# Feature tiles of the bias stage: 54 of 144 on GpSimd, 66 on VectorE, 24 on ScalarE

## The chip, the cores and the metric

The kernel runs on one core of a Trainium2 chip. A core has engines that run side by side, each with its own queue of instructions in a fixed order: TensorE (PE; its weight loads are listed apart as PEld), VectorE (DVE), ScalarE (ACT), GpSimd (POOL) and SyncE (SP), which here only issues DMA transfers. They wait for one another by semaphores. Matrix products go to PSUM, everything else lies in SBUF (both 128 partitions wide); DMA engines move data between SBUF and DRAM. The metric is device time in microseconds, taken as a median of runs; a profile of one further execution shows when each instruction ran.

## What is computed

An attention layer with a learned position bias, followed by a soft mixture of experts, all in float32. The shapes are 8 batches, 8 heads, 576 positions and 64 numbers a head. What the change touches is the bias:

```python
rel = pos[:, None] - pos[None, :]
psi_rel = log1p(abs(rel))
psi_i = log1p(maximum(pos[:, None], 1.0))
x = (psi_rel / psi_i)[..., None]          # 576 x 576 x 1
h = maximum(x @ w1 + b1, 0.0)             # 32 hidden numbers for each pair
bias = h @ w2                             # one number a head for each pair
scores = scores + bias.transpose(2, 0, 1)[None]
```

The scores then go through a softmax over the last axis and are multiplied by v; the result, 4608 rows of 512, is dispatched to 32 slots of 8 experts (two matrix products with a ReLU between), and combined again. The bias is the same for all batches, so it is computed once.

## The kernel before

**Bias stage.** The first 54 us make the bias for all heads. For a position i the hidden vector depends on the distance alone: `relu(log1p(distance) * (w1 / psi_i) + b1)`. One *feature tile* holds this for four positions (32 partitions each) and for as many distances as are needed, n of them:

- `tabs` is a table of log1p of the distances 0 to 575, the same on all partitions, loaded once; `scl` holds w1 / psi_i as a column for each tile; `cols[:, 1]` is b1, and `nb1` is -b1.
- `bias_feats(i)` (L226) makes the four tiles t = 0 to 3 of group i, that is of 16 positions. Two forms are in use: ScalarE computes `relu(scl * tabs + b1)` (L236), VectorE computes `max(scl * tabs, -b1)` (L239). The second is the first less b1; the constant that this leaves out is added later, by `bcon`, of which `bias_group` picks the column that suits the group.
- There are 36 groups: 8 in each of four blocks of 128 positions, whose biases go to `bias_m`, and 4 for the last 64 positions, which go to `bias_r`. The length n = max(base + 16, 576 - base) falls from 576 to 304 and rises again, in steps of 16 from group to group.
- `bias_group` (L245) first makes the features up to three groups ahead (`AHEAD = 3`), then multiplies the four tiles of its own group by `wbd`, which holds w2 (L260; each tile fills its own 32 columns of TensorE, in two or three pieces), lets ScalarE move the 128 x 591 result from PSUM to a tile `e` with the constant added (L264), and issues the write of `e` to DRAM on SyncE's queue (L265).
- Features and results share one pool, `wp`, of 24 buffers. A feature's buffer is free when its products are done, a result's when its write has landed. PSUM is used in four pairs of banks in turn.

Before the change ScalarE makes tile t = 0 of five groups in six (30 tiles) and VectorE everything else (114). GpSimd has nothing to do until the attention stage.

**Reading the bias back.** `load_bias(hp, c)` (L298, its DMAs at L296) reads block c of a pair of heads, shifted row by row, into SBUF: three transfers each for blocks 0 to 3 (`bm`), two for the last (`br`). They are issued on the same SyncE queue as the writes. For the first pair of heads they are in this stage, and each has to wait until the writes of its block have landed. In this stage the order of instructions on each queue, and the choice of buffers, is made by the framework's scheduler from the program's order and its own estimates; it puts the reads of a block between later writes.

**Attention and the rest.** Thirty-two units (4 pairs of heads, 8 batches) follow in an order written out by hand (`PLAIN` and `END`), under which no instruction changes place. A unit takes five rows of 128 queries; the names of its steps are S (scores, L370 and L366), t (bias added and minimum taken, L383, on VectorE), e (exponential, L390), m (sums, L398 and L399), n (normalisation by GpSimd, L312, a `tensor_scalar` of 128 x 576), T and R (transposes, L348), M (product with v, L473). Row 4 holds the last 64 queries of both heads and reads `br`; in the first unit its step t comes before that of row 3. The mixture of experts runs within the last units and after them. L655 and L653 belong to it, and are VectorE's work on 128 x 160 and 128 x 5 numbers.

Of the kernel before, what the change touches and what calls it, by code (L numbers as in the profile page):

```python
# [13 lines left out]
ALU = mybir.AluOpType  # L14
# [111 lines left out]
def body(ctx, tc, qk, v, wcol, phi, mw1, mw2, tabh, consth, out, outr):  # L126
    nc = tc.nc
# [56 lines left out]
    tabs = xp.tile([P, tabh.shape[1]], F32, name="tabs", tag="xo")  # L184
# [6 lines left out]
    scl = xp.tile([P, NJ], F32, name="scl", tag="xk")  # L191
# [15 lines left out]
    nb1 = const.tile([P, 1], F32, name="nb1")  # L207
# [3 lines left out]
    for g in range(4):  # L211
        rs = slice(32 * g, 32 * g + 32)
        nc.vector.tensor_scalar(out=wbd[rs, H * g:H * g + H], in0=cols[rs, 2:2 + H], scalar1=1.0 / QS, scalar2=None,
                                op0=ALU.mult)
# [11 lines left out]
    def bias_feats(i):  # L226
        bases, scales, _ = jobs[i]
        fb = [None] * 4
        relu = [False] * 4
        for t in range(4):  # L230
            sc = scales[t]
            n = max(bases[0] + 16, S - bases[0])
            f = fb[t] = wp.tile([P, S], F32, name="f", tag="w")[:, 0:n]
            relu[t] = t == 0 and i % 6 != 5
            if relu[t]:
                nc.scalar.activation(out=f, in_=tabs[:, 0:n], func=AF.Relu, bias=cols[:, 1:2],  # L236
                                     scale=scl[:, sc:sc + 1])
            else:
                nc.vector.tensor_scalar(out=f, in0=tabs[:, 0:n], scalar1=scl[:, sc:sc + 1], scalar2=nb1[:, 0:1],  # L239
                                        op0=ALU.mult, op1=ALU.max)  # L240
        feats[i] = fb, relu

    nb = [0]
# [1 line left out]
    def bias_group():  # L245
        i = nb[0]
        nb[0] += 1
        for j in range(i if i else 0, i + AHEAD + 1):
            if j < len(jobs) and j not in feats:
                bias_feats(j)  # L250
        bases, scales, dst = jobs[i]
        fb, relu = feats[i]
        pb = ps(i % 4)

        i0 = bases[0] + 16
        cuts = sorted({0, i0, 512, S + 15})
        for c0, c1 in zip(cuts, cuts[1:]):
            for t in (1, 2, 3, 0):
                x = fb[t][:, i0 - c1:i0 - c0][:, ::-1] if c0 < i0 else fb[t][:, c0 - i0 + 1:c1 - i0 + 1]
                nc.tensor.matmul(pb[32 * t:32 * t + 32, c0 // 512, c0 % 512:(c1 - 1) % 512 + 1], wbd, x, start=True,  # L260
                                 stop=True, tile_position=(0, 32 * t))
        e = wp.tile([P, S + 15], F32, name="e", tag="w")
        bc = bcon[:, 1 * relu[0] + 2 * relu[3]:1 * relu[0] + 2 * relu[3] + 1]
        nc.scalar.activation(out=e, in_=pb.rearrange("a x n -> a (x n)")[:, 0:S + 15], func=AF.Identity, bias=bc)  # L264
        nc.sync.dma_start(out=dst, in_=e)  # L265
# [54 lines left out]
    for i, x in enumerate(END.split()):  # L320
        n, u = x.rstrip("+").split("/")
# [707 lines left out]
```

## Time and profile before

| | us |
|---|---|
| median of 3 runs (606.54 to 610.15) | 607.62 |
| the profiled execution | 607.81 |
| its span, first to last instruction | 605.4 |
| busy: TensorE / ScalarE / VectorE / GpSimd | 582.2 / 469.8 / 414.9 / 224.6 |
| feature tiles on VectorE (114), first start to last end | 47.9 |

In the rows of the profile a line stands as L and its number, `out<-in` names the tiles written and read, and `x` the number of instructions. A group's row gives busy time in us and the mean of one instruction in ns, then the idle time of the engine before these instructions and what ended it. A row of the timeline gives start and duration in us, with runs of like instructions merged (the duration is then that of the run); in brackets stand the idle time before and who ended it. SPq is SyncE's queue issuing a DMA; when the transfer lands is told elsewhere. An instruction's duration can reach into that of the next one on its engine. The rows that matter are shown in the prediction.

### The profile page before, as it was taken

What the parts mean: (1) busy time and instruction counts of PE and PEld (TensorE: products, weight loads), DVE (VectorE), ACT (ScalarE), POOL (GpSimd) and SP (SyncE); (2) the same over time, 40 slices, a digit from 0 to 9 for tenths busy, and PEclk for the clock granted to TensorE, in tenths of its full rate; (3) what the DMA queues carried; (4) which work ended last, traced back from release to release, by engine and by line L of the source; (5) the groups of instructions that cost most, each with busy time, mean ns of one, the idle gap of its engine ahead of it and who ended that gap; (6) DMA issues with size and microseconds to landing.
All of it is one profiled execution on the core that took longest, in us unless ns stands there. A gap on an engine that the chain in (4) does not pass through costs nothing.

```text
span 605.4 us, 18911 instructions
## 1 busy us (share of the span) xinstructions
PE 582.2 (96%) x7423; PEld 370.5 (61%) x7423; DVE 414.9 (69%) x1320; ACT 469.8 (78%) x974; POOL 224.6 (37%) x336
## 2 busy tenths in 40 slices
PE   6998899999999999999999999999999999999993
PEld 4874666666666666666666666665666666653551
DVE  7997767667676667667676667677679788852233
ACT  6996888888888888888888888887877887751233
POOL 0001644455555544455555544544233422400000
PEclk9999899999999999999999999999999999999998
DMA  6778222333855544675444356522332145689997
GB/s 223 272 243 298 66 84 84 109 101 123 242 183 190 174 156 154 216 251 175 138 156 138 120 203 222 164 75 73 123 123 71 55 129 210 207 331 324 410 381 316
DMA packets 41897, 110.73 MB, mean 183 GB/s; under 512 B 7120, under 2 KB 7248, under 8 KB 41808
## 3 DMA queue, kind: packets, MB, share of 16 engines
q1 hardware_dynamic: 41808, 109.52, 53.2%
q8 instruction: 58, 0.95, 0.7%
q14 instruction: 31, 0.25, 0.1%
HBM read 82.10 MB, written 27.41 MB: 181 GB/s over the span
## 4 chain that ended last, share of the span: by engine, by line
PE 83%; DMA 6%; DVE 4%; ACT 3%; issue 1%; POOL 0%; SPq 0%; DVEq 0%; ACTq 0%; POOLq 0%
PE ps L473 25%; PE ps L370 21%; PE ps L348 17%; PE ps L260 7%; PE ps L366 6%; DMA wt<-in_moe_w_dram 5%; ACT y L390 2%; PE ps L539 1%; DMA xo<-xs 1%; PE ps L669 1%; PE ps L888 1%; DVE ob L315 1%; PE ps L921 1%; DVE y L383 0%; POOL y L312 0%
## 5 line engine op out<-in xcount | busy, mean ns | idle before, releaser
L312 POOL TENSOR_SCALAR y<-y,sm 128x576 f32<-128x576 f32 (+1 forms) x320 | 221.9, 707 | 302.1 <-DVE sm L399 246.6
L383 DVE CUSTOM_DVE_ANT_0 y<-ps,bm 128x576 f32<-128x576 f32 x256 | 185.3, 754 | 95.5 <-PE ps L348 55.2
L390 ACT ACTIVATE y<-y,mn 128x576 f32<-128x576 f32 x288 | 222.1, 772 | 28.3 <-DVE sm L398 19.3
L315 ACT COPY at<-ps 128x1024 f32<-128x1024 f32 (+3 forms) x211 | 153.9, 732 | 37.0 <-PE ps L348 28.3
L473 PE MATMUL ps<-at,v 128*64 128x320 f32 (+1 forms) x1280 | 176.4, 415 | 0.0
L370 PE MATMUL ps<-qk 64*128 64x288 f32 x1024 | 155.6, 421 | 0.1
L348 PEld LDWEIGHTS ps<-ident,y 64*128 64x128 f32 x2624 | 103.1, 139 | 56.5 <-POOL y L312 16.0
L348 PE MATMUL ps<-ident,y 64*128 64x64 f32 x2624 | 118.0, 226 | 4.1 <-POOL y L312 3.6
L473 PEld LDWEIGHTS ps<-at,v 128*64 128x64 f32 x1280 | 84.0, 137 | 60.7 <-issue 10.8
L370 PEld LDWEIGHTS ps<-qk 64*128 64x128 f32 x1024 | 90.8, 188 | 26.7 <-DVE sm L398 9.8
L390 ACT ACTIVATION_READ_ACCUMULATOR y<-y,mn 128x1 f32 x288 | 53.9, 187 | 0.0
L260 PE MATMUL ps<-f,wbd 128*32 128x79 f32 (+32 forms) x856 | 48.4, 345 | 1.7 <-DVE f L239 1.6
L239 DVE TENSOR_SCALAR f<-tabs,scl,nb 128x576 f32<-128x576 f32 (+17 forms) x114 | 47.9, 496 | 0.5 <-DMA tabs<-in_tab_dram 0.5
L315 DVE COPY at<-ps 128x256 f32<-128x256 f32 (+3 forms) x77 | 33.8, 442 | 15.3 <-PE ps L348 13.8
L260 PEld LDWEIGHTS ps<-f,wbd 128*32 128x32 f32 x856 | 33.2, 112 | 16.9 <-issue 8.1
L366 PE MATMUL ps<-qk 64*64 64x288 f32 x256 | 38.0, 415 | 0.0
L315 DVE COPY xts<-ps 128x256 f32<-128x256 f32 (+1 forms) x57 | 25.9, 455 | 12.1 <-PE ps L473 12.1
L264 ACT ACTIVATE e<-ps,bcon 128x591 f32<-128x591 f32 x36 | 26.7, 754 | 4.7 <-DMA bias_m<-e 2.1
L399 DVE RECIPROCAL sm<-sm 128x2 f32<-128x2 f32 (+1 forms) x160 | 26.5, 165 | 5.5
L398 DVE TENSOR_SCALAR sm<-sm 128x2 f32<-128x2 f32 (+1 forms) x160 | 28.3, 177 | 2.9 <-ACT y L390 2.3
L383 DVE CUSTOM_DVE_ANT_0 y<-ps,br 128x576 f32<-128x576 f32 x32 | 24.0, 750 | 1.9 <-PE ps L348 1.1
L383 DVE DVE_READ_ACCUMULATOR2_ANT mn<- 128x1 f32 x288 | 24.1, 84 | 0.0
(144 smaller groups left out, 333.5 us busy)
## 6 DMA issues: line engine op xcount, KB each, us to landing
wt<-in_moe_w_dram SPq DMA_DIRECT2D x63, 512.0 KB, 6.1
qk<-in_qk_dram SPq DMA_DIRECT2D x32, 608.0 KB, 3.8
v<-in_v_dram SPq DMA_DIRECT2D x32, 320.0 KB, 3.2
bias_m<-e SPq DMA_DIRECT2D x32, 295.5 KB, 4.2
out_dram<-ob SPq DMA_DIRECT2D x16, 512.0 KB, 5.9
xs<-xts SPq DMA_DIRECT2D x24, 288.0 KB, 4.9
xo<-xs SPq DMA_DIRECT2D x8, 864.0 KB, 5.4
bm<-bias_m SPq DMA_DIRECT2D x16, 288.0 KB, 4.4
```

The costliest lines, as they stand in the source:

```text
L239: nc.vector.tensor_scalar(out=f, in0=tabs[:, 0:n], scalar1=scl[:, sc:sc + 1], scalar2=nb1[:, 0:1], op0=ALU.mult, op1=ALU.max)
L260: nc.tensor.matmul(pb[32 * t:32 * t + 32, c0 // 512, c0 % 512:(c1 - 1) % 512 + 1], wbd, x, start=True, stop=True, tile_position=(0, 32 * t))
L264: nc.scalar.activation(out=e, in_=pb.rearrange("a x n -> a (x n)")[:, 0:S + 15], func=AF.Identity, bias=bc)
L312: nc.gpsimd.tensor_scalar(out=out, in0=y, scalar1=r, scalar2=1.0, op0=ALU.mult, op1=ALU.mult)
L315: (nc.vector.tensor_copy if eng else nc.scalar.copy)(out=out, in_=in_)
L348: nc.tensor.matmul(out, src[rs], ident[rs, rs], is_transpose=True, start=True, stop=True, tile_position=(64 * r, 0))
L366: nc.tensor.matmul(pss[0].t[rs, n, 0:HALF], x[rs, 1152:1216], x[rs, 64 + n * HALF:64 + (n + 1) * HALF], start=True, stop=True, tile_positi ...
L370: nc.tensor.matmul(pss[hh].t[:, n, 0:HALF], x[rs, 640 + p * P:640 + (p + 1) * P], x[rs, k0:k0 + HALF], start=True, stop=True, tile_positio ...
L383: nc.vector.tensor_tensor_reduce(out=d["y", p][:, hs].rearrange("a (x n) -> a x n", x=2), in0=t[:, :, 0:HALF], in1=biases[hp][p][:, hs].re ...
L390: nc.scalar.activation(out=y, in_=y, func=AF.Exp, bias=d["mn", p][:, hh:hh + 1], scale=-1.0, accum_out=d["sm", p][:, hh:hh + 1])
L398: nc.vector.tensor_scalar(out=r, in0=r, scalar1=1e-9, scalar2=None, op0=ALU.add)
L473: nc.tensor.matmul(po[64 * hh:64 * hh + 64], d["v"][:, v0:v0 + 64], main[:, :, 4 * hh + i, :] if i < 4 else rest, start=i == 0, stop=i == ...
```

## The change

Three tile positions are handed out anew in `bias_feats`. Tile t = 3 of every group, and tile t = 2 of every even group, is made by GpSimd, with the same `tensor_scalar` as VectorE's. ScalarE makes t = 0 in two groups of three in place of five of six; in the third, VectorE makes it. So GpSimd has 36 + 18 = 54 tiles, ScalarE 24, and VectorE 36 + 18 + 12 = 66. Everything else is as it was: lengths, products, results, writes, the pool of buffers.

```diff
-            relu[t] = t == 0 and i % 6 != 5
+            relu[t] = t == 0 and i % 3 != 2
             if relu[t]:
                 nc.scalar.activation(out=f, in_=tabs[:, 0:n], func=AF.Relu, bias=cols[:, 1:2],
                                      scale=scl[:, sc:sc + 1])
             else:
-                nc.vector.tensor_scalar(out=f, in0=tabs[:, 0:n], scalar1=scl[:, sc:sc + 1], scalar2=nb1[:, 0:1],
-                                        op0=ALU.mult, op1=ALU.max)
+                eng = nc.gpsimd if t == 3 or t == 2 and i % 2 == 0 else nc.vector
+                eng.tensor_scalar(out=f, in0=tabs[:, 0:n], scalar1=scl[:, sc:sc + 1], scalar2=nb1[:, 0:1], op0=ALU.mult,
+                                  op1=ALU.max)
```

## The prediction

> **What bounds the kernel now.** I read the page first, for the instructions that the change touches.
>
> ```profile
> span 605.4 us, 18911 instructions
> ...
> L239 DVE TENSOR_SCALAR f<-tabs,scl,nb 128x576 f32<-128x576 f32 (+17 forms) x114 | 47.9, 496 | 0.5 <-DMA tabs<-in_tab_dram 0.5
> ```
>
> VectorE's 114 feature tiles fill 47.9 us with no gap after the first: 47.9 / 114 = 0.42 us from one to the next (the mean of 496 ns is longer, since each instruction begins some 76 ns before the last one is recorded as ended). Next come the busy times of the stage by stretches; behind the length stand PE, PEld, DVE, ACT and POOL, then clock, DMA share and GB/s.
>
> ```profile
> 10.00:20.00 10.00, 10.00 (x209) 7.75 (x201) 10.00 (x24) 9.63 (x15) 0.00 (x0) 1.00 0.58 221
> 20.00:30.00 10.00, 10.00 (x203) 8.16 (x203) 10.00 (x28) 9.50 (x17) 0.00 (x0) 1.00 0.82 290
> 30.00:40.00 10.00, 10.00 (x202) 7.77 (x196) 10.00 (x26) 9.72 (x17) 0.00 (x0) 1.00 0.79 273
> 40.00:50.00 10.00, 10.00 (x163) 5.18 (x160) 10.00 (x24) 8.28 (x12) 0.00 (x0) 1.00 0.71 221
> ```
>
> VectorE never rests, GpSimd never works, ScalarE is nearly full. TensorE shows full too, but its records overlap and it consumes what VectorE hands over. So VectorE sets the pace of the features. A second chain runs beside it: SyncE's queue, which writes each group's result to DRAM and reads the biases of the first head pair back.
>
> ```profile
> 22.27 0.32 SPq L296 DMA_DIRECT2D bm<-bias_m  x1
> ...
> 33.17 0.32 SPq L296 DMA_DIRECT2D bm<-bias_m  x1
> ...
> 44.29 0.32 SPq L296 DMA_DIRECT2D bm<-bias_m  x1
> ...
> 55.47 1.31 SPq L296 DMA_DIRECT2D bm<-bias_m  x3
> 59.31 1.15 SPq L296 DMA_DIRECT2D br<-bias_r  x2
> ```
>
> Each of the first four is the first read of a block of eight groups (`bm`), and the last row reads the rest (`br`). A read waits at the head of the queue until the last write of its block has landed, and later writes wait behind it:
>
> ```profile
> SPq L296 <- DMA bias_m<-e: 9.8, 6, 4.2
> ```
>
> The blocks follow one another at 10.9, 11.1 and 11.2 us. In between the DMA engines are full (share 1.01 to 1.04; columns as above):
>
> ```profile
> 24.00:31.00 7.00, 7.00 (x150) 5.86 (x152) 7.00 (x21) 6.70 (x12) 0.00 (x0) 1.00 1.01 380
> 35.00:42.00 7.00, 7.00 (x134) 4.85 (x132) 7.00 (x18) 6.76 (x12) 0.00 (x0) 1.00 1.03 391
> ...
> 50.00:54.00 4.00, 4.00 (x60) 2.14 (x58) 2.50 (x6) 2.32 (x4) 0.00 (x0) 1.00 1.04 403
> ```
>
> So this chain runs at the pace of the transfers and of the queue's waits, and it is slower than the features: eight groups cost VectorE 8 x 114 / 36 x 0.42 = 10.6 us. Where the two meet is seen on VectorE in the first attention unit:
>
> ```profile
> 55.09 0.76 DVE L383 CUSTOM_DVE_ANT_0 y<-ps,bm 128x576 f32<-128x576 f32 x1 [2.59 <-PE ps L370]
> ...
> 62.70 0.76 DVE L383 CUSTOM_DVE_ANT_0 y<-ps,br 128x576 f32<-128x576 f32 x1 [0.30 <-DMA br<-bias_r]
> ```
>
> The unit starts when the features are done (55.09), yet its row at 62.70 waits 0.30 us for the last bias read. **The end of the stage is set twice**, by the features and, 0.30 us later, by the DMA chain. What follows is one fixed order of work on a full TensorE, so I carry a shift of that row to the end one for one.
>
> **The change, part by part.** VectorE loses 48 tiles, ScalarE loses 6, GpSimd gets 54. A tile's length is max(base + 16, 576 - base), 304 to 576, on average 440 over any of the three engines' shares. Their prices by length:
>
> ```profile
> L239 DVE TENSOR_SCALAR f<-tabs,scl,nb 128x576 f32<-128x576 f32 x7 | 3.6, 571 | 0.5 <-DMA tabs<-in_tab_dram 0.5
> ...
> L239 DVE TENSOR_SCALAR f<-tabs,scl,nb 128x304 f32<-128x304 f32 x7 | 2.5, 426 | 0.0
> ```
> ```profile
> L312 POOL TENSOR_SCALAR y<-y,sm 128x576 f32<-128x576 f32 x288 | 212.3, 750 | 256.0 <-DVE sm L399 227.0 <-PE ps L348 5.3 <-DVE sm L398 4.6
> L312 POOL TENSOR_SCALAR y<-y,sm 128x64 f32<-128x64 f32 x32 | 10.3, 322 | 46.1 <-DVE sm L399 19.6 <-ACT y L390 7.9 <-ACT at L315 6.3
> ```
>
> VectorE: 145 ns over 272 columns, 0.533 ns a column, so 0.23 us of streaming at 440 in its 0.42. GpSimd: 428 ns over 512 columns, 0.836 ns a column and 268 ns fixed, so 0.636 us at 440; back to back each begins 27 ns early (two in 1.47 below), so 0.61. L312 also has two scalar operations with a column operand, and I take its price for the new tiles.
>
> If the two engines did not disturb each other, GpSimd would need 54 x 0.61 = 32.9 us, VectorE 66 x 0.42 = 27.7, and ScalarE 60 instructions (24 tiles, 36 results) at 9.63 / 15 = 0.64, 38.5 us. ScalarE would bind: 9.4 us less than 47.9. That is the lower bound. But they do disturb each other. Small VectorE operations in the attention stage show it:
>
> ```profile
> L398 DVE TENSOR_SCALAR sm<-sm x160: 144/160/921, 57.6 to 525.4; 128x2 f32<-128x2 f32 x128, 128x1 f32<-128x1 f32 x32
> L655 DVE TENSOR_TENSOR ck<-ck,km x8: 325/326/614, 457.8 to 547.7; 128x160 f32<-128x160 f32 x8
> ```
> ```profile
> 406.88 0.54 DVE L398 TENSOR_SCALAR sm<-sm 128x2 f32<-128x2 f32 x1 [0.60 <-ACT y L390]
> ...
> 482.58 0.17 DVE L653 TENSOR_SCALAR km<-km 128x5 f32<-128x5 f32 x1
> ...
> 483.01 0.45 DVE L655 TENSOR_TENSOR ck<-ck,km 128x160 f32<-128x160 f32 x1
> ```
> ```profile
> 406.65 1.47 POOL L312 TENSOR_SCALAR y<-y,sm 128x576 f32<-128x576 f32 x2
> ...
> 482.52 1.55 POOL L312 TENSOR_SCALAR y<-y,sm 128x576 f32<-128x576 f32 x2 [0.82 <-DVE sm L399]
> ```
>
> At 406.88 an operation of 0.16 us lasts 0.54: it ends at 407.42, some 0.02 us after the first of the two GpSimd instructions (406.65 + 0.75). It got in between the two, and the pair took no longer for it. At 483.01 a longer one (160 columns) ends 0.17 us after the first GpSimd instruction, and the pair takes 1.55 in place of 1.47. So VectorE waits out a running GpSimd instruction, then streams, and about the first 0.1 us of the next GpSimd instruction is free of the conflict. A feature tile that has waited streams 0.23 + 0.02 = 0.25 us after GpSimd's end and delays the next GpSimd instruction by about 0.15. A pair, one tile on each, thus takes 0.61 + 0.15 = 0.76 us. With 54 pairs and 12 more VectorE tiles: 54 x 0.76 + 12 x 0.42 = **46.1 us, 1.8 less than 47.9**.
>
> The upper bound is no overlap at all: 54 x 0.636 + 66 x 0.42 = 62.1 us, 14.2 more. I choose the pair price, since it is read from the same GpSimd instruction; the bounds stay for the range. The Trainium skill, SBUF — State Buffer, "Who interferes with whom", has the harder rule: a float32 `tensor_scalar` between SBUF tiles can take both VectorE ports, one of them is GpSimd's, and whichever instruction comes first holds it whole while the other "fully blocks". The trace agrees that VectorE waits out GpSimd (921 against 160 ns), but not that the next GpSimd instruction gives up its whole length; by the rule the sum would be the upper bound.
>
> ScalarE's 6 tiles less save 6 x 0.64 = 3.8 us on an engine that is not the one that ends the stage: nothing by itself. TensorE and the writes keep their work; a group still needs four tiles.
>
> **Where the 1.8 us go.** The DMA chain starts with the eighth group's write (the read at 22.27 waits for it). Groups 0 to 7 are long (mean 520 columns): before, 25 VectorE tiles at 0.277 + 0.185 = 0.46, 11.5 us; after, 12 pairs at 0.68 + 0.20 = 0.88 and 2 tiles more, 11.4 us. The chain starts where it did, its blocks are paced by full DMA engines, and the `br` read lands where it did. The features' gain comes later, in the short middle groups, and turns into a longer wait at the 62.70 row: 0.30 becomes some 2 us. If features came later, only 0.30 us of cover exists; beyond it the cost is one for one.
>
> Sum: -0.1 (the chain's start) on a profiled execution of 607.81 us, which is 2.4 over its span; the median of the runs shown is 0.2 below it, so 607.81 - 0.1 - 0.2 = **607.5 us**. Its own range, with the chain's start moving by up to 2 us either way, is 605 to 610.
>
> **The rivals.** *Slower: the two engines exclude each other more than the small rows show.* Place: every pair of the stage. It decides from a pair price of (47.9 + 0.3 - 5.0) / 54 = 0.80 us on, only 0.04 above mine. If GpSimd's free 0.1 us is lost, a pair is 0.61 + 0.25 = 0.86, the features take 51.4 us, and the time is 607.6 + 3.2 = 610.8; at the upper bound it is 607.6 + 14.2 - 0.3 = 621.5. For it: the small operations hold VectorE for nanoseconds, a feature tile for a quarter of a microsecond, and two VectorE tiles in a row may keep GpSimd out. Against it: the 406.65 pair, which let VectorE in at no cost. 0.21, about half of it near each end. The rule of the Trainium skill's SBUF page is the case of the far end.
>
> *Faster: the DMA chain shortens too.* ScalarE, 9.63 of 10 us busy at 10 to 20, has one tile less before the eighth group, and the order of SyncE's queue in this stage is the framework's plan, not written by hand; if the plan lets one more write go ahead of each read, each of four blocks saves a write of 302 KB at 391 GB/s, 0.77 us. With that tile's 0.64 us: 3.7 less, 603.9 us, if the features keep up, which needs pairs of (47.9 - 3.7 - 5.0) / 54 = 0.73 us. For it: full DMA engines only between waits. Against: nothing in the change touches the queue's code. 0.16.
>
> *The new wait is for buffers.* Features and results share 24 buffers, and a result's is free only when its write has landed; ScalarE already waited for that:
>
> ```profile
> 50.32 1.40 ACT L264 ACTIVATE e<-ps,bcon 128x591 f32<-128x591 f32 x2 [1.86 <-DMA bias_m<-e]
> ```
>
> If a GpSimd tile gets such a buffer, GpSimd's later tiles queue behind it, TensorE waits for them, and ScalarE for TensorE: 1.9 us in each of three blocks, 607.6 + 5.6 - 0.3 = 613. Against: no feature tile waited so before. 0.06.
>
> **How the numbers follow.** Forecast 0.57, exclusion 0.21, shorter chain 0.16, buffers 0.06. About 0.5% (3 us) is what a measurement can tell from no change. The forecast lies within it; the shorter chain is beyond it; exclusion (from 610.8 on) and buffers are slower: faster 0.16, same 0.57, slower 0.27. The range, 603 to 617, leaves out the upper half of the exclusion (0.11) and the far end of the shorter chain (some 0.05).
>
> **What would show it.** VectorE's feature tiles should lengthen beyond 571 ns, each ending just after a GpSimd instruction, and GpSimd's lie near 0.6 to 0.8 us. The last feature should end near 51 us in place of 52.5 (13.52 + 38.98 in the row below), the reads of the blocks should stay near 22.3, 33.2, 44.3 and 55.5, and the `br` row near 62.7 should show some 2 us of waiting for DMA.
>
> ```profile
> 13.52 38.98 DVE L239 TENSOR_SCALAR f<-tabs,scl,nb 128x480 f32<-128x480 f32 x95
> ```
>
> I am wrong about the lock if the features end after 53 us, and about the cover if the `br` row moves with them while the reads move too.

## The result, and the profile after

The changed kernel takes 664.7 us (median of 4 runs, 662.86 to 666.96), beside 608.76 us for the kernel before. The ratio is **1.092, 95% interval 1.087 to 1.098**: 56 us slower. The forecast was 607.5 us and no change that can be told. The profiled execution took 662.86 us. Ratios and intervals, here and below, leave out the few runs that fell in a slower state of the chip; medians do not.

The page of the changed kernel shows the loss at once (first the span, then the chain that ended last by engine, then groups of instructions as before; from here on line numbers are those of each kernel's own file):

```profile
span 660.7 us, 18941 instructions
...
PE 75%; POOL 12%; issue 4%; ACT 3%; DVE 3%; DMA 1%; SPq 0%; POOLq 0%; DVEq 0%; ACTq 0%
...
L240 POOL TENSOR_SCALAR f<-tabs,scl,nb 128x576 f32<-128x576 f32 (+17 forms) x54 | 104.0, 1939 | 3.6 <-DMA tabs<-in_tab_dram 3.6
...
L261 PEld LDWEIGHTS ps<-f,wbd 128*32 128x32 f32 x856 | 32.2, 119 | 74.5 <-POOL f L240 58.6
L240 DVE TENSOR_SCALAR f<-tabs,scl,nb 128x576 f32<-128x576 f32 (+17 forms) x66 | 41.0, 666 | 52.0 <-PE ps L261 43.3
```

GpSimd was 0% of the chain before and is now 12% of 660.7, some 79 us. Its 54 tiles take 104.0 us, 1939 ns each, where the prediction had 636. TensorE's weight loads wait 58.6 us for them. VectorE is idle for 52.0 us, mostly because TensorE has not yet given buffers back. VectorE's tiles end soon enough: the weight loads wait 50 times for a GpSimd tile and once for a VectorE tile. GpSimd itself is never idle between its first tile and its last, so it sets the pace of the stage.

Two stretches show GpSimd's price by itself, since VectorE made no tile beside the 304 columns of the first and beside any of the second (groups of one shape; the 320-column tile still had a VectorE tile beside its start and is not used):

```profile
L240 POOL TENSOR_SCALAR f<-tabs,scl,nb 128x320 f32<-128x320 f32 x1 | 1.5, 1494 | 0.0
L240 POOL TENSOR_SCALAR f<-tabs,scl,nb 128x304 f32<-128x304 f32 x1 | 1.4, 1369 | 0.0
```
```profile
L240 POOL TENSOR_SCALAR f<-tabs,scl,nb 128x560 f32<-128x560 f32 x2 | 4.4, 2224 | 0.0
L240 POOL TENSOR_SCALAR f<-tabs,scl,nb 128x576 f32<-128x576 f32 x1 | 2.3, 2277 | 0.0
```

From 304 to 576 columns the tile grows by 908 ns: 3.34 ns a column and 354 ns fixed, 1.82 us at 440 columns. The rows of L312, from which the prediction took its price, gave 0.836 ns a column. So of the 1.94 us a tile about 0.12 us are the neighbours' doing; nearly everything is the instruction itself.

The first attention unit on VectorE shows that the loss goes to the end one for one:

```profile
111.52 0.76 DVE L384 CUSTOM_DVE_ANT_0 y<-ps,bm 128x576 f32<-128x576 f32 x1 [14.57 <-PE ps L371]
...
118.75 0.75 DVE L384 CUSTOM_DVE_ANT_0 y<-ps,br 128x576 f32<-128x576 f32 x1
```

The unit starts at 111.52 in place of 55.09, 56.4 us later, and the span is 55.3 us longer. The row that reads the last biases no longer waits for DMA: the writes now come so slowly that the chain on SyncE's queue keeps up.

### The profile page after: what moved, and what is told of

Same layout as the page of the kernel before. It is cut to its first block, busy times and chain, and to the rows that moved or that the text cites. A ratio compares the mean times of both kernels' runs of the same rounds, so it can differ in the third digit from the quotient of the medians.

```text
span 660.7 us, 18941 instructions
## 1 busy us (share of the span) xinstructions
PE 602.7 (91%) x7423; PEld 370.2 (56%) x7423; DVE 407.7 (62%) x1272; ACT 467.9 (71%) x968; POOL 327.8 (50%) x390
## 4 chain that ended last, share of the span: by engine, by line
PE 75%; POOL 12%; issue 4%; ACT 3%; DVE 3%; DMA 1%; SPq 0%; POOLq 0%; DVEq 0%; ACTq 0%
PE ps L474 24%; PE ps L371 19%; PE ps L349 15%; POOL f L240 12%; PE ps L367 5%; PE ps L889 2%; PE ps L845 2%; ACT y L391 2%; PE ps L540 1%; PE ps L670 1%; PE ps L922 1%; DVE ob L316 1%; ACT at L316 1%; DMA bias_m<-e 1%; DVE y L384 1%
## 5 line engine op out<-in xcount | busy, mean ns | idle before, releaser
L240 POOL TENSOR_SCALAR f<-tabs,scl,nb 128x576 f32<-128x576 f32 (+17 forms) x54 | 104.0, 1939 | 3.6 <-DMA tabs<-in_tab_dram 3.6
L261 PE MATMUL ps<-f,wbd 128*32 128x79 f32 (+32 forms) x856 | 70.1, 374 | 36.6 <-POOL f L240 33.7
L261 PEld LDWEIGHTS ps<-f,wbd 128*32 128x32 f32 x856 | 32.2, 119 | 74.5 <-POOL f L240 58.6
L240 DVE TENSOR_SCALAR f<-tabs,scl,nb 128x576 f32<-128x576 f32 (+17 forms) x66 | 41.0, 666 | 52.0 <-PE ps L261 43.3
L316 DVE COPY xts<-ps 128x256 f32<-128x256 f32 (+1 forms) x57 | 25.9, 454 | 11.3 <-PE ps L474 11.2
```

The source lines that it names most:

```text
L240: eng.tensor_scalar(out=f, in0=tabs[:, 0:n], scalar1=scl[:, sc:sc + 1], scalar2=nb1[:, 0:1], op0=ALU.mult, op1=ALU.max)
L316: (nc.vector.tensor_copy if eng else nc.scalar.copy)(out=out, in_=in_)
```

## The experiments

Six kernels in the changed form with another operation in GpSimd's tiles, then one with fewer tiles on GpSimd, then kernels in the form of before: one that takes work from the features, and variants. Each of the six leaves out of GpSimd's tiles what its operation does not do (the rectifier, b1 or the multiplication). Times are device microseconds; where there is no interval, one run was made, and "before" is the median of the kernel before in the same batch.

| run | GpSimd's 54 tiles | one tile, median us | time | before | ratio |
|---|---|---|---|---|---|
| the change | multiply by column, maximum with column | 1.95 | 664.7 | 608.76 | 1.092 (1.087 to 1.098) |
| mul_one | multiply by column, multiply by 1.0 | 0.76 | 607.06 | 608.33 | 0.997 (0.995 to 0.999) |
| mul_col | multiply by two columns | 0.85 | 609.84 | 608.33 | |
| mul_add | multiply by column, add column | 0.84 | 608.18 | 609.08 | |
| max_imm | multiply by column, maximum with 0.0 | 1.82 | 657.3 | 608.33 | |
| max_mul | maximum with 0.0, multiply by column | 1.82 | 662.88 | 609.08 | |
| max_only | maximum with 0.0 alone | 1.36 | 634.4 | 609.08 | |

**mul_one: the borrowed form itself.** VectorE's tiles keep the maximum.

```diff
-                eng.tensor_scalar(out=f, in0=tabs[:, 0:n], scalar1=scl[:, sc:sc + 1], scalar2=nb1[:, 0:1], op0=ALU.mult,
-                                  op1=ALU.max)
+                if eng is nc.gpsimd:
+                    eng.tensor_scalar(out=f, in0=tabs[:, 0:n], scalar1=scl[:, sc:sc + 1], scalar2=1.0,
+                                      op0=ALU.mult, op1=ALU.mult)
+                else:
+                    eng.tensor_scalar(out=f, in0=tabs[:, 0:n], scalar1=scl[:, sc:sc + 1], scalar2=nb1[:, 0:1],
+                                      op0=ALU.mult, op1=ALU.max)
```

> GpSimd's 54 tiles are multiplied by their column and by 1.0 (the form of L312, whose price the prediction borrowed) in place of the maximum with -b1: the rectifier of these tiles is left out, VectorE's and ScalarE's tiles are unchanged. The changed kernel's GpSimd tiles took 1369 ns (304 columns) to 2277 ns (576) where no VectorE instruction ran beside them, 3.34 ns a column, in place of 0.836 borrowed. Theory A, the price lies in the second operation (maximum): GpSimd's tiles take 0.52 to 0.75 us, the features end near 51 us, the time is 605 to 611. Theory B, it lies in the second operand being a column: the same as A here, 605 to 611. Theory C, it lies in the place (another input tile that three engines read, not in place, VectorE beside it): GpSimd's tiles stay at 1.4 to 2.3 us and the time at 655 to 670.

Measured: 607.06 us, ratio 0.9972 (0.9949 to 0.9994). A tile (least, median, greatest ns):

```profile
L241 POOL TENSOR_SCALAR f<-tabs,scl x54: 524/757/1337, 4.7 to 49.7; 128x576 f32<-128x576 f32 x3, 128x560 f32<-128x560 f32 x3, 128x544 f32<-128x544 f32 x3, 128x528 f32<-128x528 f32 x3
```

Theory C, the place, falls: the same input, output, neighbours and count give 0.76 us once the operation is another. The last tile starts at 49.7 and is done by 50.6, where the prediction had 51. This run is the changed kernel at the price that the prediction assumed.

**mul_col, max_imm: the operation or the second column.** In both only the GpSimd branch of the code above differs:

```diff
mul_col:
+                    eng.tensor_scalar(out=f, in0=tabs[:, 0:n], scalar1=scl[:, sc:sc + 1], scalar2=nb1[:, 0:1],
+                                      op0=ALU.mult, op1=ALU.mult)
max_imm:
+                    eng.tensor_scalar(out=f, in0=tabs[:, 0:n], scalar1=scl[:, sc:sc + 1], scalar2=0.0,
+                                      op0=ALU.mult, op1=ALU.max)
```

> GpSimd's 54 tiles are multiplied by both columns (second operation a multiplication by -b1 in place of the maximum; the rectifier of these tiles is left out). Theory A (the maximum is dear): 0.52 to 0.75 us a tile, time 605 to 611. Theory B (the second column is dear): 1.4 to 2.3 us a tile, time 655 to 670. Theory C (the place): as B.

> GpSimd's 54 tiles take the maximum with the constant 0.0 in place of the column -b1 (b1 is left out of these tiles). Theory A (the maximum is dear): 1.4 to 2.3 us a tile, time 655 to 670. Theory B (the second column is dear): 0.52 to 0.75 us a tile, time 605 to 611. Theory C (the place): as A.

The same view of the two kernels, mul_col first:

```profile
L241 POOL TENSOR_SCALAR f<-tabs,scl,nb x54: 657/852/1466, 4.7 to 51.8; 128x576 f32<-128x576 f32 x3, 128x560 f32<-128x560 f32 x3, 128x544 f32<-128x544 f32 x3, 128x528 f32<-128x528 f32 x3
```
```profile
L241 POOL TENSOR_SCALAR f<-tabs,scl x54: 1297/1824/2801, 4.7 to 100.8; 128x576 f32<-128x576 f32 x3, 128x560 f32<-128x560 f32 x3, 128x544 f32<-128x544 f32 x3, 128x528 f32<-128x528 f32 x3
```

Two columns and two multiplications are cheap (median 0.85 us, some 0.1 over mul_one); a maximum with a constant is nearly as dear as the change's (1.82 against 1.95). Both times lie in the ranges of theory A. Theory A stands, theory B falls but for that 0.1 us.

**max_only, mul_add, max_mul: the maximum, or any two different operations.**

```diff
max_only:
+                    eng.tensor_scalar(out=f, in0=tabs[:, 0:n], scalar1=0.0, scalar2=None, op0=ALU.max)
mul_add:
+                    eng.tensor_scalar(out=f, in0=tabs[:, 0:n], scalar1=scl[:, sc:sc + 1], scalar2=cols[:, 1:2],
+                                      op0=ALU.mult, op1=ALU.add)
max_mul:
+                    eng.tensor_scalar(out=f, in0=tabs[:, 0:n], scalar1=0.0, scalar2=scl[:, sc:sc + 1],
+                                      op0=ALU.max, op1=ALU.mult)
```

> GpSimd's 54 tiles take one operation, the maximum of the table with 0.0; the multiplication is left out of them. Theory A1, the maximum itself is dear on GpSimd: about 3.3 ns a column, 1.2 to 2.2 us a tile, time 645 to 660. Theory A2, two different operations in one instruction are dear, whichever they are: 0.5 to 0.8 us a tile, time 604 to 611.

> GpSimd's 54 tiles are multiplied by their column and b1 is added: the product before the rectifier, which is left out of these tiles. Theory A1 (the maximum is dear): as with two multiplications by columns, 0.65 to 1.0 us a tile, time 605 to 612. Theory A2 (two different operations are dear): 1.4 to 2.3 us a tile, time 650 to 665.

> GpSimd's 54 tiles take the maximum with 0.0 first and are then multiplied by their column (b1 is left out of these tiles, and the order of the operations is turned round). Theory A1: 1.2 to 2.2 us a tile, time 650 to 660. Theory A2: the same. If only a maximum in second place is dear: 0.5 to 0.8 us a tile and 604 to 611.

In the same order:

```profile
L241 POOL TENSOR_SCALAR f<-tabs x54: 999/1360/2128, 4.8 to 77.5; 128x576 f32<-128x576 f32 x3, 128x560 f32<-128x560 f32 x3, 128x544 f32<-128x544 f32 x3, 128x528 f32<-128x528 f32 x3
```
```profile
L241 POOL TENSOR_SCALAR f<-tabs,scl,cols x54: 660/838/1402, 5.1 to 51.2; 128x576 f32<-128x576 f32 x3, 128x560 f32<-128x560 f32 x3, 128x544 f32<-128x544 f32 x3, 128x528 f32<-128x528 f32 x3
```
```profile
L241 POOL TENSOR_SCALAR f<-tabs,scl x54: 1292/1818/2787, 4.6 to 101.0; 128x576 f32<-128x576 f32 x3, 128x560 f32<-128x560 f32 x3, 128x544 f32<-128x544 f32 x3, 128x528 f32<-128x528 f32 x3
```

A multiplication and an addition are two different operations and cost what two multiplications do: A2 falls. The maximum is dear in first place as in second. Alone, its tile lies in the range that A1 named (median 1.36 us), but the time, 634.4, lies under its 645; the tile is still about 1.8 times that of two multiplications. With a multiplication beside it the tile takes 0.46 us more (1.82). So the maximum itself is dear on GpSimd. No run has a multiplication alone, so what one adds beside another is not known, and why the maximum is dear is not shown; no run looks inside the instruction. max_mul's time, 662.88, lies above its range and 5.6 us above max_imm's, though the tiles are the same; TensorE's mean granted clock was 0.978 there, 0.987 in max_imm, which may be the reason and was not tested.

**few: the whole computation with 18 tiles on GpSimd.** Against the changed kernel:

```diff
-            relu[t] = t == 0 and i % 3 != 2
+            relu[t] = t == 0 and i % 6 != 5
-                eng = nc.gpsimd if t == 3 or t == 2 and i % 2 == 0 else nc.vector
+                eng = nc.gpsimd if t == 3 and i % 2 == 0 else nc.vector
```

> The whole computation, with GpSimd making only the fourth tile of every even group, 18 tiles, ScalarE 30 as before and VectorE 96. GpSimd alone needs 18 x 1.94 = 35 us, less than the stage has. If VectorE and GpSimd do not slow each other, VectorE needs 96 x 0.42 = 40 us and the time is near that of the run with 78 VectorE tiles, 602 to 605. If they slow each other as in the changed kernel, where VectorE's tiles lasted 666 ns in the mean in place of 496, VectorE's some 70 tiles beside GpSimd cost 0.17 us more each, the features end within 2 us of where they did before, and the time is 605 to 611.

Measured: 611.39 us beside 609.08, ratio 1.0025 (0.9990 to 1.0060): no gain. The groups of the stage:

```profile
L240 DVE TENSOR_SCALAR f<-tabs,scl,nb 128x576 f32<-128x576 f32 (+17 forms) x96 | 50.1, 600 | 0.9 <-DMA tabs<-in_tab_dram 0.9
L240 POOL TENSOR_SCALAR f<-tabs,scl,nb 128x576 f32<-128x576 f32 (+17 forms) x18 | 39.2, 2183 | 11.1 <-PE ps L261 6.1 <-DMA tabs<-in_tab_dram 3.7 <-DMA bias_m<-e 1.0
```

VectorE has 18 tiles less than the 114 and is busy longer, 50.1 us in place of 47.9: 0.52 us a tile in place of 0.42. GpSimd's tiles take 2.18 us, where 1.82 is the price without neighbours. The engines slow each other by at least as much as the split saves. This is as the second expectation had it, but a little worse: the features end 2.4 us later than before (54.9 in place of 52.5) where it allowed 2, and the time lies just above its 611.

**cover: a quarter of the features left out, to test the DMA chain.** Against the kernel before; the third tile of each group stands in for the fourth:

```diff
+            if t == 3:
+                fb[t] = fb[2]
+                continue
             f = fb[t] = wp.tile([P, S], F32, name="f", tag="w")[:, 0:n]
```

> The kernel before, with the fourth tile of each group not computed: the third tile stands in for it in the products, so VectorE has 78 tiles in place of 114 and everything behind the features is the same work. It tests the other step of the prediction, that faster features are worth next to nothing because the chain of writes and reads on the DMA queue sets the same end 0.30 us later. If so: the first attention row starts some 5 us earlier, the row that reads the last biases still waits for DMA until about 60 to 63 us, and the time is 603 to 608.5. If the features alone set the end: ScalarE's 66 instructions of 0.64 us bind at 42 us, the stage ends 5 to 6 us earlier, and the time is 600 to 603.

Measured: 603.04 us beside 608.33, ratio 0.9921 (0.9901 to 0.9941). SyncE's queue, the first read of each block and the reads of the rest:

```profile
21.73 0.32 SPq L299 DMA_DIRECT2D bm<-bias_m  x1
...
31.66 0.32 SPq L299 DMA_DIRECT2D bm<-bias_m  x1
...
41.75 0.32 SPq L299 DMA_DIRECT2D bm<-bias_m  x1
...
51.76 1.27 SPq L299 DMA_DIRECT2D bm<-bias_m  x3
54.84 1.15 SPq L299 DMA_DIRECT2D br<-bias_r  x2
```

The blocks follow at 9.9, 10.1 and 10.0 us in place of 10.9, 11.1 and 11.2, and the last reads are issued 4.5 us earlier, so the chain does not stand still when the features come earlier. VectorE's last feature tile ended 7.8 us earlier (44.7 in place of 52.5). Not all of that arrives, because another engine now ends the stage. ScalarE's last result before, then its last results and the first row and the `br` row of attention in cover:

```profile
53.83 0.75 ACT L264 ACTIVATE e<-ps,bcon 128x591 f32<-128x591 f32 x1 [1.17 <-PE ps L260]
```
```profile
45.92 3.43 ACT L267 ACTIVATE e<-ps,bcon 128x591 f32<-128x591 f32 x5
...
49.71 0.76 DVE L386 CUSTOM_DVE_ANT_0 y<-ps,bm 128x576 f32<-128x576 f32 x1 [5.00 <-ACT e L267]
...
58.26 0.76 DVE L386 CUSTOM_DVE_ANT_0 y<-ps,br 128x576 f32<-128x576 f32 x1
```

Before, ScalarE waits for products; here it is busy without a break from 12 us on, its last result ends at 49.35, and attention's first row waits 5.00 us for it. That row comes 5.4 us earlier (49.71 in place of 55.09) and the time falls by 5.3. This is what the second expectation described: it put 42 us on ScalarE's 66 instructions, and they take 43 (6.16 to 49.35). The `br` row shows no wait for DMA, where the cover theory expected one, though only just: the second of the two reads, issued at 55.40, landed 2.8 us later, at 58.2. So the chain moved along with the results, by about 4.4 us. The time, 603.04, lies on the border of the two ranges and decides nothing by itself.

**act36: the same relief without GpSimd.** Against the kernel before:

```diff
-            relu[t] = t == 0 and i % 6 != 5
+            relu[t] = t == 0
```

> The whole computation with nothing on GpSimd in the bias stage: ScalarE makes the first tile of every group, 36, and VectorE 108. VectorE needs 108 x 0.42 = 45.4 us, ScalarE 72 x 0.64 = 46.1, both under the 47.9 of before. If the time follows the features by about 0.7 us a us, as it did with 78 VectorE tiles (5.3 us of 7.8): 1.3 us less, 606 to 608. If the two engines' waits for each other eat it: no change, 608 to 609.

Measured: 608.27 us beside 607.97, ratio 1.0007 (0.9982 to 1.0031). The features end 1.2 us earlier (51.3), and nothing of it can be told in the time. One tile position given wholly to ScalarE buys nothing here.

**gpq, gpq36, gpqcover: the reads on GpSimd's queue.** The reads of the first pair of heads are issued by GpSimd, alone and together with act36 and cover (the flag `first_pair` is true for `hp == 0`; the lines that pass it on are left out here).

```diff
-        nc.sync.dma_start(out=out, in_=x)
+        (nc.gpsimd if first_pair else nc.sync).dma_start(out=out, in_=x)
```

> The kernel before with one thing moved: the reads of the biases of the first pair of heads are issued by GpSimd's queue, idle at that time, in place of SyncE's, so no write waits behind a read. If the end of the stage is set by the features and by the DMA chain 0.30 us later, as the prediction has it, the last bias read lands earlier, the row that reads it no longer waits, and the time falls by 0.3 us: no change that can be told, 607 to 609. If the writes' delay costs more than that row shows, 603 to 606.

> Both of the last two changes together. If the queue is what takes the rest of the features' gain, the features' 1.8 us come through whole: 1.8 to 2.1 us less than before, 606 to 607. If not, as with 36 tiles on ScalarE alone.

> The kernel before with the fourth tile of each group not computed (the third stands in for it) and the reads of the first pair of heads on GpSimd's queue. With the reads on SyncE's queue the features ended 7.8 us earlier and the time fell by 5.3. If the queue held the rest back, the time now falls by 7 to 8 us, 600 to 602; if the transfers themselves did (full DMA engines), it stays at 602.5 to 604.

Measured: gpq 613.41 us, ratio 1.0086 (1.0071 to 1.0100); gpq36 614.72, 1.0102 (1.0070 to 1.0133); gpqcover 610.59, 1.0014 (0.9979 to 1.0050). All miss what either theory named. One cause is a single row. GpSimd's queue in gpq, and VectorE's end of its feature tiles in the same kernel:

```profile
23.35 29.48 POOL L296 DMA_DIRECT2D bm<-bias_m  x1 [22.04 <-DMA bias_m<-e]
```
```profile
49.69 3.02 DVE L239 TENSOR_SCALAR f<-tabs,scl,nb 128x560 f32<-128x560 f32 x6
```

Issuing one read, which takes about 0.54 us when undisturbed (the median of the twelve), lasted 29.48 us, from 23.35 to 52.83: until VectorE's unbroken train of feature tiles was over (49.69 + 3.02 = 52.71). The other reads then crowd together. The same first read lasted 26.80 us in gpq36, and one lasted 9.82 in gpqcover. A second difference goes with it: from 55 to 80 us TensorE's granted clock was 0.80 in all three, 0.93 in the kernel before; how the loss divides between the two is not shown. So these three runs do not tell what they were made for, how much of the features' gain SyncE's queue takes; as a whole that stays open. No version was found that beats the kernel before with the whole computation.

## Why the prediction was wrong

**The step that failed** is one sentence: "L312 also has two scalar operations with a column operand, and I take its price for the new tiles." L312 multiplies twice, by a column and by the constant 1.0; the new tile multiplies and takes a maximum. The term "GpSimd would need 54 x 0.61 = 32.9 us" measured 104.0. The trace of before shows no maximum on GpSimd at all, so this was an operation that it does not price. Of the bounds, 38.5 us was ScalarE's own work and 62.1 us was built from the borrowed price. They bounded the conflict between the engines and left the operation unbounded. That is why the result lies far outside the range of 603 to 617, and why the slower rival, even at its far end (621.5), named the wrong cause.

**The pair price was right for the form it was read from.** In mul_one, which has the price that was assumed, the two engines go in step over the first half of the stage (GpSimd's row, then VectorE's):

```profile
4.69 20.91 POOL L241 TENSOR_SCALAR f<-tabs,scl 128x576 f32<-128x576 f32 x28 [3.39 <-DMA tabs<-in_tab_dram]
```
```profile
4.54 21.60 DVE L244 TENSOR_SCALAR f<-tabs,scl,nb 128x576 f32<-128x576 f32 x30 [0.55 <-DMA tabs<-in_tab_dram]
```

That is 20.91 / 28 = 0.75 us a pair, where 0.76 was worked out, and the features end at 50.6 where 51 was forecast. One figure beside it was misread: the 921 ns in the row of L398 is an operation at 68.69, behind three VectorE copies and beside GpSimd's memory fills (L204); beside a multiplication of L312 the longest is 635 ns, at 419.86. The 0.54 and 0.45 us from which the price was made are right.

The time of mul_one, 607.06 us, is nearer to the forecast's 607.5 than the mechanism deserves: the kernel before took 608.33 in that batch, so 1.3 us were gained where 0.1 was forecast. VectorE's row:

```profile
61.85 0.76 DVE L388 CUSTOM_DVE_ANT_0 y<-ps,br 128x576 f32<-128x576 f32 x1 [1.26 <-DMA br<-bias_r]
```

It waits 1.26 us in place of 0.30 (forecast: some 2), and stands at 61.85 in place of 62.70. So of the 1.9 us by which the features came earlier, about half was taken by the DMA chain, not nearly all. ScalarE's last result and SyncE's queue in mul_one show one place where it was taken:

```profile
52.08 0.75 ACT L269 ACTIVATE e<-ps,bcon 128x591 f32<-128x591 f32 x1 [0.29 <-PE ps L265]
```
```profile
53.48 0.32 SPq L301 DMA_DIRECT2D bm<-bias_m  x1
53.85 0.90 SPq L270 DMA_DIRECT2D bias_r<-e  x2
```

The last result was ready at 52.83, 1.75 us earlier than before (54.58). Its write is the second of the two at 53.85, behind a read that waits, so it went out only some 0.3 us earlier than before.

**"What follows is one fixed order of work": right.** The first row of attention moved by 56.4 us, the span by 55.3. The difference is not explained.

**The cover was judged too tight.** "The chain starts where it did, its blocks are paced by full DMA engines": in cover its start moved by 0.5 us and its blocks by 1 us each. In mul_one the read of the fourth block stands at 53.48 in place of 55.47 and the `br` reads at 58.33 in place of 59.31, so the `br` row moved while the reads moved too, which is the prediction's own sign that the cover was wrong. Full DMA engines inside a block did not mean that the block's length was theirs; waits at either end, which depend on when results arrive, belong to it too. The queue's wait for the blocks' last writes, 9.8 us before, is 4.1 in cover.

**The rivals.** Exclusion: not what cost the time, about 0.12 of 1.94 us a tile. In mul_one, where GpSimd's tiles are cheap, it costs what the pair price said. Buffers: GpSimd did wait for a write's landing in mul_one, but not in the changed kernel. The shorter chain did not occur in the changed kernel. It did in cover and mul_one, but there the results came earlier and the framework's order of writes and reads was another one too; no run separates the two.

**The pages beside the runs.** The prediction used a page for the conflict and none for the operation. The Trainium skill, GPSIMD Engine Reference, "Engine selection", names add, mul and max in one row and says that one-input work of this kind on GpSimd is "roughly line-rate". The row puts no figure to that; as one rate for the three operations it fits the runs for multiplications and additions (0.76 to 0.85 us a tile) and not for the maximum (1.36 alone, 1.82 to 1.95 with a multiplication). The rule of the Trainium skill's page SBUF — State Buffer that the prediction set against the rows, that a GpSimd instruction holds the port whole, gave a sum of 62.1 us for the features; mul_one measured some 46 (4.5 to 50.6).

## What to carry to other kernels

An instruction's price belongs to its operation, not to its name and shape: before work is moved to another engine, find that operation on that engine in a trace, and where there is none, treat its price as unknown and let the range say so. On GpSimd here, a `tensor_scalar` with a multiplication and a maximum took 1.82 to 1.95 us where one with two multiplications took 0.76 to 0.85. When an engine is full and other work ends close behind it, a change that speeds the first brings less than its own gain: here 1.3 us of 1.9 (mul_one), 5.3 of 7.8 (cover) and nothing that can be told of 1.2 (act36). What it can bring at most is measured by taking the work away before anything is moved.

## What the runs showed beyond that

**VectorE passes a slow GpSimd instruction.** The start of the changed kernel, GpSimd and VectorE:

```profile
4.89 10.54 POOL L240 TENSOR_SCALAR f<-tabs,scl,nb 128x576 f32<-128x576 f32 x4 [3.58 <-DMA tabs<-in_tab_dram]
```
```profile
4.73 6.29 DVE L240 TENSOR_SCALAR f<-tabs,scl,nb 128x576 f32<-128x576 f32 x10 [0.77 <-DMA tabs<-in_tab_dram]
```

Ten VectorE tiles are done in 6.29 us while GpSimd works on its first three: 0.63 us each in place of about 0.47 at these lengths, but none waits for a whole GpSimd instruction of over 2 us. The multiplications of L312, in the rows that the prediction showed, did make VectorE wait to their end, and in mul_one the two engines took turns.

**An unbroken train on VectorE can shut GpSimd's DMA issue out**, for 29.48 us in gpq. The Trainium skill, SBUF — State Buffer, "SBUF: two separate sides", describes this trap, in which GpSimd cannot write descriptors while VectorE holds the port; the trace of gpq agrees and shows that there it lasted as long as the train did. It need not: in gpqcover the first three reads were issued in 2.13 us, from 22.17 on, while VectorE made its tiles without a break from 19.86 to 24.01. What decides is not shown. GpSimd's arithmetic was not shut out in that way in any run; the longest of its tiles without a maximum took 1.47 us, in mul_col.
